# Layer 1 of a gated mixer: tokens normalised and transposed on the chip instead of column means and row scaling, and the whole program in a hand-written order

## The chip, the cores and the metric

The kernel runs on one core of a Trainium2 chip. The metric is the device time of one execution in microseconds (us); before the change it is 401.55 us (median of three runs, 401.23 to 402.5). Engines are called as the profile calls them: PE multiplies matrices (PEld loads its weights), DVE and ACT work on vectors, POOL is the general engine, and SP only issues transfers (DMAs). Each engine takes its instructions in the order of its own queue.

## What is computed

The input is 2048 tokens of 448 columns. An MLP mixer `b` and a state-space convolution `a` are mixed by a gate per token:

```python
g = sigmoid((x * gate_w).sum(-1, keepdims=True))
a = ssm(x)                         # long convolution, plus x * D_skip
h = gelu(layernorm(x) @ w1)        # layer 1: 448 -> 448
hs = concat(shift(h0, +1), shift(h1, -1), shift(h2, +2), shift(h3, -2)) @ w2
x1 = x + hs
b = x1 + gelu(layernorm(x1) @ w3) @ w4    # layer 2: 448 -> 1792 -> 448
out = g * a + (1 - g) * b
```

`layernorm` subtracts the token's mean and divides by the root of its variance; `shift` moves a quarter of the columns along the tokens by one or two places.

## The kernel before

The tokens are cut into 4 **blocks** of 512 (`TB`), a block into 4 **tiles** of 128. The work is a list of 72 **units**: 16 of layer 1 (block by block, the column groups 0, 2, 1, 3), then 56 of layer 2 (block by block, 14 groups of 128 hidden columns). A unit n has a **first product** (`first`, L378), 11 matmuls of 512 columns that leave a group of hidden columns in PSUM, then a gelu on ACT (L394, L396), its split in a rounded high part `uh` (L402, ACT) and a low part `ul` (L406, DVE), and a **second product** (`second`, L433), 12 matmuls that add the group to four sums of a tile each. All products use high and low parts of both factors, so inputs and weights are split in the same way: the high part by an ACT copy, the low part by a DVE (or POOL) subtraction.

**Step** n of the loop issues the first product of unit n+2 and the second product of unit n, and between them whatever tables `before`, `between`, `after` and `late` hold for n. They are filled by `at(n, fn, ...)`: `sp3(c, k)` splits half a chunk of `w3` (L216, L217), `sp4` two groups of `w4`, `stats_b` and `rstd` the statistics of the layer norm, `norm` and `norm_t` the normalising and transposing of a tile for layer 2 (L320, L334), `ssm_moment` and others the state-space part, whose scans run on DVE from step 28.

Layer 1 of before needs no normalised tokens. The mean over the columns is taken out of `w1` (`col_means`, L630, and `split_w1`, L634), the raw transposed tokens `xT` come from memory and are split (`split_xt`, L309 and L311), and what comes out of the first product is scaled per token by `rb` (L393). `rb` holds the tokens' reciprocal deviations as rows: `rstd_rows` (L294) transposes them on PE. The program up to step 27 is written in an order that a scheduler may change; from step 28 (`OWN`) the written order holds on each engine.

Of the kernel before, what the change touches and what calls it, by code (L numbers as in the profile page):

```python
# [31 lines left out]
OWN = 28  # L32
# [12 lines left out]
def gated_mix_kernel(tc, x, xT, w1, w2, w3, w4, par, logdt, dskip, ident, parg, uflip, lags, out):  # L45
    nc = tc.nc
    with tc.tile_pool(name="keep", bufs=1) as keep:
        xs = keep.tile([128, L // 128, D], F32, name="xs")
        gg = keep.tile([128, L // 128], F32, name="gg")
        okm = keep.tile([128, 16], I32, name="okm")  # L50
        with ExitStack() as ctx:
            mixer_and_small_steps(ctx, tc, xs, gg, okm, x, xT, w1, w2, w3, w4, par, logdt, dskip, ident, out)
# [121 lines left out]
def mixer_and_small_steps(ctx, tc, xs, gg, okm, x, xT, w1, w2, w3, w4, par, logdt, dskip, ident, out):  # L174
# [69 lines left out]
    nc.gpsimd.memset(cm, 1.0 / D)  # L244
    w1r = big.tile([128, 4, 4, GW], F32, name="w1r", tag="w4al")
    w2r = big.tile([G, 4, D], F32, name="w2r", tag="w4ah")
    raw[0] = room([128, 4, XW], "raw")
    nc.scalar.dma_start(w1r[:, 0], w1[:, 0])
    for k in range(4):
        nc.sync.dma_start(raw[0][:, k, :], xT[:, k, 0:XW])  # L250
    nc.sync.dma_start(w1r[:, 2], w1[:, 2])
    load_x(0, 1)
    load_x(1, 3)
    nc.sync.dma_start(w1r[:, 1], w1[:, 1])
    load_x(3, NT + 1)
    nc.sync.dma_start(idt, ident)
    nc.sync.dma_start(w1r[:, 3], w1[:, 3])
    nc.sync.dma_start(w2r, w2)
    load_xt(1)
    load_x(NT + 1, 2 * NT + 1)  # L260
    nc.gpsimd.memset(one, 1.0)
    nc.gpsimd.memset(nu, 0.0)
    nc.gpsimd.memset(zero, 0.0)
    nc.gpsimd.memset(carry, 0.0)
    nc.gpsimd.memset(rb[:, 0:HALO], 0.0)
    nc.gpsimd.memset(rb[:, L + HALO:L + 2 * HALO], 0.0)


    def stats_b(j0, j1):
        b6 = wk.tile([128, NT + 1, 6], F32, name="b6")  # L270
        for j in range(j0, j1):
            nc.vector.bn_stats(b6[:, j - j0, :], xs[:, j, :])  # L272
        for j in range(j0, j1):
            nc.vector.bn_aggr(st[:, j, :], b6[:, j - j0, :])

    def rstd(r, j0, j1):

        v, t = (wk.tile([128, NT + 1], F32, name=n)[:, :j1 - j0] for n in "vt")
        y = r[:, j0:j1]
        nc.vector.tensor_scalar(v, st[:, j0:j1, 1], EPS, None, op0=OP.add)  # L280
        nc.vector.tensor_scalar(y.bitcast(I32), v.bitcast(I32), -0.5, float(0x5f3759df), op0=OP.mult, op1=OP.add)
        for _ in range(3):
            nc.vector.tensor_mul(t, y, y)
            nc.vector.scalar_tensor_tensor(t, t, -0.5, v, op0=OP.mult, op1=OP.mult)
            nc.vector.scalar_tensor_tensor(y, t, 1.5, y, op0=OP.add, op1=OP.mult)

    def rstd2(j0, j1):
        rstd(r2, j0, j1)
        nc.vector.scalar_tensor_tensor(nm[:, j0:j1], st[:, j0:j1, 0], -1.0, r2[:, j0:j1], op0=OP.mult, op1=OP.mult)

    def rstd_rows(j0, j1, bank="misc"):
        p = ps.tile([128, TB], F32, name="misc", tag=bank, bufs=2 if bank == "misc" else 1)
        for j in range(j0, j1):
            nc.tensor.transpose(p[:, (j - j0) * 128:(j - j0 + 1) * 128], r1[:, j:j + 1].to_broadcast([128, 128]), idt)  # L294
        nc.scalar.activation(rb[:, HALO + j0 * 128:HALO + j1 * 128], p[:, :(j1 - j0) * 128], AF.Copy)
# [8 lines left out]
    def split_xt(b, k0, k1):  # L304
        if k0 == 0:
            hl_tiles(("a", b))
        h, lo = XH["a", b], XL["a", b]
        for k in range(k0, k1):
            nc.scalar.activation(h[:, k, :], raw[b][:, k, :], AF.Copy)  # L309
            if k < 3:  # L310
                nc.vector.tensor_sub(lo[:, k, :], raw[b][:, k, :], f32(h[:, k, :]))  # L311
            else:
                nc.vector.tensor_sub(h[64:, 3, :], raw[b][64:, 3, :], f32(h[64:, 3, :]))

    XN = {}

    def norm(b, i, early=False):
        j = NT * b + i
        xn = XN[b, i] = wk.tile([128, 512], F32, name="xn", tag="xn")
        nc.scalar.activation(xn[:, :D], xs[:, j, :], AF.Identity, bias=nm[:, j:j + 1], scale=r2[:, j:j + 1])  # L320
        if early:
            nc.vector.tensor_copy(xn[:, D:], xn[:, D - 64:D])
        else:
            nc.scalar.activation(xn[:, D:], xs[:, j, D - 64:], AF.Identity, bias=nm[:, j:j + 1], scale=r2[:, j:j + 1])

    def norm_t(b, i):
        j = NT * b + i
        if i == 0:
            hl_tiles(("d", b))
        h, lo = XH["d", b], XL["d", b]  # L330
        xn = XN.pop((b, i))
        p = ps.tile([128, 4, 128], F32, name="misc")
        for k in range(4):
            nc.tensor.transpose(p[:, k, :], xn[:, k * 128:(k + 1) * 128], idt)  # L334
        t = slice(i * 128, (i + 1) * 128)
        nc.scalar.activation(h[:, :, t], p, AF.Copy)
        NT_[b, i] = p

    NT_ = {}

    def norm_lo(b, i):
        h, lo, p, t = XH["d", b], XL["d", b], NT_.pop((b, i)), slice(i * 128, (i + 1) * 128)
        nc.vector.tensor_sub(lo[:, :, t], p[:, :3, :], f32(h[:, :3, t]))
        nc.vector.tensor_sub(h[64:, 3, t], p[64:, 3, :], f32(h[64:, 3, t]))

# [11 lines left out]
    def first(n, bank="p1", fill=0):  # L357
# [11 lines left out]
        p = P1[n] = ps.tile([128, TB], F32, name="p1", tag=bank, bufs=2)  # L369
# [7 lines left out]
        for q, (a_, b_) in enumerate(seq):  # L377
            nc.tensor.matmul(p[:m], a_, b_, start=(q == 0), stop=(q == len(seq) - 1))  # L378
            if q < 4:
                warm_up(fill)  # L380

    def act_head(n, later=False):
        kind, b, i = units[n]
        m = G if kind == "a" else 128
        lo = UL[n] = wk.tile([128, TB], F32R, name="ul", bufs=3)
# [3 lines left out]
        if kind == "a":  # L389
            if i == 0 or (i == 1 and b == NB - 1):  # L390
                logits(p, b, i)
            o = b * TB + HALO - SHIFT[i]
            nc.vector.tensor_mul(u[:m], p[:m], rb[:m, o:o + TB])  # L393
            nc.scalar.activation(u[:m], u[:m], AF.Gelu_apprx_tanh)  # L394
        else:
            nc.scalar.activation(u[:m], p[:m], AF.Gelu_apprx_tanh)  # L396
        if not later:
            act_copy(n)
# [17 lines left out]
    def second(n):  # L416
# [64 lines left out]
    def ssm_par(q):  # L481
        pk[q] = room([128, 2, 4, NS], f"pk{q}")
        nc.sync.dma_start(pk[q], par[:, 2 * q:2 * q + 2])

    def ssm_exp(q):
        nc.scalar.activation(pk[q][:, :, 0, :], pk[q][:, :, 0, :], AF.Exp)
        if q:
            return
# [4 lines left out]
    CM = {}  # L493
# [7 lines left out]
    def ssm_moment(k, m):  # L501
# [5 lines left out]
        w = wk.tile([128, 2, NS], F32, name="w", tag="xn")  # L507
        nc.vector.tensor_mul(w, c, t[:, 0:2, :])  # L508
        nx = wk.tile([128, 2, NS], F32, name="nx", tag="u")
# [29 lines left out]
    def ssm_load(b):  # L539
        ZS[b] = wk.tile([128, 4, TB], F32, name="zs", tag="rawc" if b % 2 else "rb", bufs=1)  # L540
# [45 lines left out]
    def ssm_queue():  # L586
# [6 lines left out]
        ssm_load(0)  # L593
        ssm_load(1)
# [25 lines left out]
    def run(when, n):  # L620
        for fn, a in when.pop(n, []):
            fn(*a)


    pm = ps.tile([128, 4, G], F32, name="pm", tag="misc")

    def col_means(g):
        for k in range(4):
            r = 64 if k == 3 else 128
            nc.tensor.matmul(pm[:, g, :], cm[:r].to_broadcast([r, 128]), w1r[:r, g, k, :G],  # L630
                             start=(k == 0), stop=(k == 3))

    def split_w1(g):
        nc.vector.tensor_tensor(w1r[:, g, :, :G], w1r[:, g, :, :G], pm[:, None, g, :].to_broadcast([128, 4, G]),  # L634
                                OP.subtract)
        split(w1h[:, g], w1l[:, g], w1r[:, g], nc.gpsimd if g else None)

    w4p, w3r = {}, {}
# [7 lines left out]
    def ld3(c):  # L646
        t = cols3(c)
        w3r[c] = stage([128, 4, t.stop - t.start], w3[:, :, t])
# [177 lines left out]
```

## Time and profile before

| what | value |
|---|---|
| median of three runs | 401.55 us |
| the profiled execution: time | 402.19 us |
| the profiled execution: span, first to last instruction | 400.4 us |
| granted clock, mean | 0.996 |
| PE busy, share of the span | 388.0 us, 97% |
| DVE busy | 307.1 us, 77% |
| ACT busy | 203.2 us, 51% |
| POOL busy | 57.2 us, 14% |
| start of the first product of unit 0 | 9.78 us |
| start of the first product of unit 4 (the first of block 1) | 32.95 us |
| start of the first product of unit 16 (the first of layer 2) | 97.31 us |
| end of the last second product | 393.54 us |

The span lacks some 1.8 us of the execution's time, which lie around it. A row of the profile gives line, engine, operation, output<-inputs, the shape, how often, the busy time and the mean of one in ns; a row of a timeline gives start, duration, engine, line and so on; L numbers are lines of the kernel before unless a text says "new line".

### The profile page before, as it was taken

The page shows a single profiled execution, that of the slowest core. Times are in us where ns is not written, and L with a number is a line of the kernel's source. Part 1 is how long each engine was busy: PE and PEld are TensorE (multiplying, and loading weights), DVE is VectorE, ACT ScalarE, POOL GpSimd, SP SyncE. Part 2 cuts the span into 40 slices and gives each one's busy share as a digit, 9 for nine tenths or more (in the row PEclk, how much of TensorE's full clock was granted, in tenths as well). Part 3 has the DMA queues.
Part 4 walks back from the last instruction along what each step waited for, and adds up shares of the span by engine and source line. Part 5 has one row for each costly group of instructions (what it writes and reads, how often), then busy time and mean ns, then how long its engine had stood idle before and what let it go on. Part 6 is the DMA issues. An engine that isn't in the chain of part 4 may idle for free.

```text
span 400.4 us, 5167 instructions
## 1 busy us (share of the span) xinstructions
PE 388.0 (97%) x1851; PEld 330.3 (82%) x1851; DVE 307.1 (77%) x581; ACT 203.2 (51%) x340; POOL 57.2 (14%) x127
## 2 busy tenths in 40 slices
PE   7999899999999999999999999999999999999993
PEld 3678788788888888888888888888888888888892
DVE  3689999989983387289999795997778778788222
ACT  4183667595696532275556524566266334442120
POOL 1260000000000000043025321242133301000000
PEclk9999999999999999999999999999999999999998
DMA  8991523613453000000000150000052002000002
GB/s 267 315 362 35 190 83 130 206 46 77 167 145 66 2 0 2 1 0 2 1 2 0 46 152 0 0 2 1 31 127 42 2 0 93 0 0 2 0 1 97
DMA packets 12903, 26.93 MB, mean 67 GB/s; under 512 B 1094, under 2 KB 6358, under 8 KB 12618
## 3 DMA queue, kind: packets, MB, share of 16 engines
q1 hardware_dynamic: 12730, 26.33, 21.2%
q8 instruction: 16, 0.26, 0.3%
q10 hardware_dynamic: 144, 0.23, 0.2%
q14 instruction: 13, 0.11, 0.1%
HBM read 22.88 MB, written 3.68 MB: 66 GB/s over the span
## 4 chain that ended last, share of the span: by engine, by line
PE 87%; DVE 6%; DMA 2%; ACT 2%; issue 1%; DVEq 0%; ACTq 0%
PE p L378 41%; PE acc L433 40%; PE misc L334 2%; PE misc L570 2%; DMA raw<-w_in 1%; DVE b L272 1%; DMA w1r<-w_in 1%; DVE ul L406 1%; PE pw L666 1%; PE pm L630 1%; DVE xl L311 1%; PE misc L294 1%; DVE w3l L217 1%; DVE uf L393 1%; ACT xh L309 0%
## 5 line engine op out<-in xcount | busy, mean ns | idle before, releaser
L396 ACT ACTIVATE uf<-p 128x512 f32<-128x512 f32 x56 | 33.5, 598 | 141.8 <-PE p L378 138.0
L406 DVE TENSOR_TENSOR ul<-uf,uh 128x512 fp32r<-128x512 f32 (+1 forms) x72 | 50.7, 705 | 36.6 <-ACT uh L402 36.4
L378 PE MATMUL p<-xh,w3h 128*128 128x512 f32 x224 | 61.2, 395 | 0.0
L378 PE MATMUL p<-xh,w3l 128*128 128x512 f32 x224 | 60.8, 393 | 0.0
L433 PE MATMUL acc<-w4h,uh 128*128 128x448 f32 x224 | 59.9, 372 | 0.0
L558 DVE TENSOR_TENSOR_SCAN z<-z,carry,zero 128x512 f32<-128x512 f32 x48 | 59.9, 1269 | 0.0
L433 PE MATMUL acc<-w4h,ul 128*128 128x448 f32 x224 | 58.2, 364 | 0.0
L433 PE MATMUL acc<-w4l,uh 128*128 128x448 f32 x224 | 58.1, 364 | 0.0
L378 PEld LDWEIGHTS p<-xh,w3l 128*128 128x128 f32 x224 | 42.1, 188 | 9.9
L378 PE MATMUL p<-xl,w3h 128*128 128x512 f32 x168 | 47.9, 394 | 0.0
L378 PEld LDWEIGHTS p<-xh,w3h 128*128 128x128 f32 x224 | 42.1, 188 | 6.7
L560 POOL COPY carry<-z 128x1 f32<-128x1 f32 x60 | 28.0, 470 | 137.1 <-DVE z L558 136.0
L402 ACT ACTIVATE uh<-uf 128x512 fp32r<-128x512 f32 (+1 forms) x72 | 45.4, 631 | 1.5
L433 PEld LDWEIGHTS acc<-w4l,uh 128*128 128x128 f32 x224 | 42.0, 188 | 3.2
L433 PEld LDWEIGHTS acc<-w4h,ul 128*128 128x128 f32 x224 | 42.0, 188 | 3.2
L433 PEld LDWEIGHTS acc<-w4h,uh 128*128 128x128 f32 x224 | 40.6, 188 | 4.4
L558 DVE TENSOR_TENSOR_SCAN z<-z,carry 128x512 f32<-128x512 f32 x32 | 41.0, 1283 | 2.0
L548 ACT ACTIVATE z<-zs,nu 128x512 f32<-128x512 f32 x64 | 41.0, 713 | 0.0
L547 POOL COPY z<-carry 128x1 f32<-128x1 f32 x48 | 20.6, 473 | 136.1 <-DVE w L508 107.3
L378 PEld LDWEIGHTS p<-xl,w3h 128*128 128x128 f32 x168 | 31.5, 188 | 7.3
L578 DVE SCALAR_TENSOR_TENSOR xs<-misc,gg,xs 128x448 f32<-128x448 f32 x16 | 10.2, 678 | 13.6 <-PE misc L570 13.6
L433 PE MATMUL acc<-w2h,uh 112*128 112x448 f32 x64 | 19.9, 371 | 0.0
(121 smaller groups left out, 493.4 us busy)
## 6 DMA issues: line engine op xcount, KB each, us to landing
zs<-xT_in SPq DMA_DIRECT2D x4, 1024.0 KB, 6.4
out_dram<-xs SPq DMA_DIRECT2D x16, 224.0 KB, 2.0
raw<-xT_in SPq DMA_DIRECT2D x3, 1032.0 KB, 11.7
raw<-w_in SPq DMA_DIRECT2D x3, 1024.0 KB, 5.5
raw<-w_in SPq DMA_DIRECT2D x3, 896.0 KB, 4.9
pk<-par_in SPq DMA_DIRECT2D x2, 1024.0 KB, 5.9
xs<-x_in SPq DMA_DIRECT2D x2, 896.0 KB
raw<-xT_in SPq DMA_DIRECT2D x4, 258.0 KB, 4.5
```

The lines of the kernel that those rows point to most:

```text
L334: nc.tensor.transpose(p[:, k, :], xn[:, k * 128:(k + 1) * 128], idt)
L378: nc.tensor.matmul(p[:m], a_, b_, start=(q == 0), stop=(q == len(seq) - 1))
L396: nc.scalar.activation(u[:m], p[:m], AF.Gelu_apprx_tanh)
L402: nc.scalar.activation(UH[n][:m], UF[n][:m], AF.Copy)
L406: nc.vector.tensor_sub(UL[n][:m], UF.pop(n)[:m], f32(UH[n][:m]))
L433: nc.tensor.matmul(ACC[j], (UL if p == 2 else UH)[n][:m, t], wl if p == 1 else wh, start=s and p == 0, stop=e and p == 2)
L547: nc.gpsimd.tensor_copy(z4[:, m, 0:1], carry[:, k, m:m + 1])
L548: nc.scalar.activation(z4[:, m, 1:], ZS[b][:, k, :], AF.Copy, scale=nu[:, k, m:m + 1])
L558: nc.vector.tensor_tensor_scan(z, z, up, carry[:, k, m:m + 1], OP.add, OP.add)
L560: nc.gpsimd.tensor_copy(carry[:, k, m:m + 1], z[:, TB - 1:])
L570: nc.tensor.transpose(p[:, k * 128:(k + 1) * 128], ZS[b][:, k, i * 128:(i + 1) * 128], idt)
L578: nc.vector.scalar_tensor_tensor(r, p[:, :D], gg[:, j:j + 1], r, op0=OP.mult, op1=OP.add)
```

## The change

Layer 1 is done as layer 2 is: each tile is normalised (`norm`, ACT, with a copy of 64 columns on POOL), transposed on PE (`norm_t`, four 128x128 transposes), and split (`norm_hi`, `norm_lo`). `cm`, `col_means`, `rb`, `rstd_rows`, `split_xt`, the row scaling and the loads of `xT` for layer 1 go. The shifts reach over a block's edge by two columns: `halo` copies them between neighbouring blocks on POOL (four small copies each time), `edge` fills the two outer ends with zeros on ACT. The gate's logit is now read from a product with normalised tokens, so `gates` puts it back (three DVE operations, and the sum of `gate_w`, which `gate_sum` loads and adds). The low parts of `w1` and `w2` are taken on DVE, not POOL. Layer 1 has its own statistics (`st1`, `r1`, `nm1`).

The whole program is put under the written order, where before only the steps from 28 were. In a step the order is now: `ul` of unit n+1, `before`, first product and gelu of unit n+2, `between`, copy to `uh`, `after`, the scans' share, `late`, second product of unit n. `stats`, `rstd` and `ln` are generators, which `mix` deals out in turn; what isn't a generator in a table is issued first. The scaling of the first scan step, which stood ahead of the mask that fills `nu` (at 136.65 us, the mask's last instruction at 172.19 us), is put behind it.

```diff
+    def norm(kind, b, i, eng):
+        ...
+        nc.scalar.activation(xn[:, :D], xs[:, j, :], AF.Identity, bias=m[:, j:j + 1], scale=r[:, j:j + 1])
+        if eng is nc.scalar:
+            nc.scalar.activation(xn[:, D:], xs[:, j, D - 64:], AF.Identity, bias=m[:, j:j + 1], scale=r[:, j:j + 1])
+        else:
+            eng.tensor_copy(xn[:, D:], xn[:, D - 64:D])
...
+    def norm_lo(kind, b, i):
+        h, lo, p, t = XH[kind, b], XL[kind, b], PT.pop((kind, b, i)), cols(kind, i)
+        nc.vector.tensor_sub(lo[:, :, t], p[:, :3, :], f32(h[:, :3, t]))
+        nc.vector.tensor_sub(h[64:, 3, t], p[64:, 3, :], f32(h[64:, 3, t]))
+
+    def halo(b):
+        for X in (XH, XL):
+            u, v = X["a", b - 1], X["a", b]
+            nc.gpsimd.tensor_copy(u[:, :, TB + HALO:], f32(v[:, :, HALO:2 * HALO]))
+            nc.gpsimd.tensor_copy(v[:, :, :HALO], f32(u[:, :, TB:TB + HALO]))
...
-            nc.vector.tensor_mul(u[:m], p[:m], rb[:m, o:o + TB])
-            nc.scalar.activation(u[:m], u[:m], AF.Gelu_apprx_tanh)
+        nc.scalar.activation(u[:m], p[:m], AF.Gelu_apprx_tanh)
...
+    def gate_sum():
+        t = wk.tile([128, D], F32, name="gt", tag="uf")
+        nc.sync.dma_start(t, gateb)
+        nc.vector.tensor_reduce(sg, t, axis=AX.X, op=OP.add)
...
-    warm_up(5)
-    col_means(0)
-    split_w1(0)
-    split_xt(0, 0, 4)
-    warm_up(3)
-    first(0, fill=2)
+    warm_up(28)
...
+    mix([stats(st1, 0, 4)])
+    nc.scalar.activation(w1h[:, 0], w1r[:, 0], AF.Copy)
+    mix([rstd(st1, r1, nm1, 0, 4)])
...
+    for i in range(4):
+        norm("a", 0, i, nc.gpsimd)
+        norm_t("a", 0, i, banks[i])
+        warm_up(1)
+        if i < 2:
+            norm_hi("a", 0, i, False)
+            norm_lo("a", 0, i)
+    for i in (2, 3):
+        norm_hi("a", 0, i)
+        norm_lo("a", 0, i)
+    first(0)
...
+    for b, n in ((2, 2), (3, 5)):
+        h = NT * b + (2 if b > 2 else 0)
+        if b > 2:
+            at(n, stats, st1, NT * b, h)
+        at(n + (b > 2), ln, st1, r1, nm1, NT * b, h, NT * b + 4)
+        for i in range(NT):
+            n = 4 * b - 5 + i // 2
+            at(n, norm, "a", b, i, nc.gpsimd, when=before)
+            n = 4 * b - 5 + i // 2 * 2
+            at(n, norm_t, "a", b, i, when=between)
+            at(n, norm_hi, "a", b, i, when=between)
+            at(n, norm_lo, "a", b, i, when=late)
+            if i == 0:
+                at(n, halo, b, when=late)
+    at(9, edge, 3, TB + HALO)
...
+    for c, m0, m1, n, w in ((0, 4, 6, None, None), (2, 12, 13, 7, "raw"), (1, 9, 11, None, None), (3, 14, 15, 11, "raw")):
+        if w:
+            at(n, ld3, c, w)
+        at(m0, sp3, c, 0)
+        at(m1, sp3, c, 2)
...
-    with tc.manual_schedule():
-        for n in range(OWN, len(units)):
+    for n in range(len(units)):
```

What the order of the instructions is, at three places. The first is DVE where the statistics of the last block of layer 1 become reciprocal deviations. Before, the chain (L280 to L285, `r_82` or `r_83`) is threaded between other rows: the split of `w3` (L217), the row scaling (L393), the low part `ul` (L406).

```order
L272 BN_STATS b_678<-xs 128x6
L284 SCALAR_TENSOR_TENSOR t<-t,v 128x4 [waits DVE_49]
L217 TENSOR_TENSOR w3l<-raw,w3h 128x2x512 [waits DMAHW7_49]
L393 TENSOR_TENSOR uf<-p_558,rb 112x512 [waits Activation_49]
L285 SCALAR_TENSOR_TENSOR r_82<-t,r_82 128x4 [waits DVE_49]
L274 BN_AGGR st<-b_678 128x2
L217 TENSOR_TENSOR w3l<-raw,w3h 128x2x512
```

Now, in step 6, one half chunk of `w3` stands first, and waits for ACT; two tiles' statistics and then the whole chain (new lines 267 to 278, twelve operations) follow without anything between.

```order
L402 TENSOR_TENSOR ul<-uf,uh 112x512 [waits Activation_49]
L218 TENSOR_TENSOR w3l<-raw,w3h 128x2x512 [waits Activation_49]
L257 BN_STATS b_674<-xs 128x6 x2
L260 BN_AGGR st_78<-b_674 128x2 [waits DVE_49] x2
L267 TENSOR_SCALAR v<-st_78 128x4 [waits DVE_49]
L269 TENSOR_SCALAR r_85<-v 128x4 [waits DVE_49]
L272 TENSOR_TENSOR t<-r_85 128x4 [waits DVE_49]
```

So the chain, whose result the tiles 12 and 13 are normalised with, moved behind a split whose high part comes from ACT. The second place is ACT in the same steps. Before, between the gelu of a unit (L394) and its `uh` (L402) stand the high parts of the raw tokens (L309) and the rows `rb` (L295); `p_558` is unit 8's.

```order
L295 ACTIVATE rb<-misc 128x512 [waits PE_49]
L394 ACTIVATE uf<-uf 112x512 [waits DVE_49]
L309 ACTIVATE xh<-raw 128x516
L402 ACTIVATE uh<-uf 112x512 [waits Activation_49]
L458 ACTIVATE lr<-p_558 18x512 [waits PE_49]
```

Now (`p_652` is unit 8's) the high part of `w3` comes behind gelu, logit rows and `uh` of unit 8, and the normalising of tiles 12 and 13 (new line 308) behind that, ahead of the gelu of unit 9.

```order
L392 ACTIVATE uf<-p_652 112x512 [waits DVE_49,PE_49]
L456 ACTIVATE lr<-p_652 18x512 [waits Pool_49]
L398 ACTIVATE uh<-uf 112x512 [waits Activation_49]
L217 ACTIVATE w3h<-raw 128x2x512
L308 ACTIVATE xn<-xs,nm_79,r_85 128x448 [waits DMAHW0_49,DVE_49,Pool_49]
L308 ACTIVATE xn<-xs,nm_79,r_85 128x448 [waits DMAHW0_49,Activation_49]
L392 ACTIVATE uf<-p_712 112x512 [waits PE_49]
```

So in this stretch ACT no longer has loaded tokens to split, and its normalising stands between two units. The third place is PE between the first product of unit 9 and the second product of unit 7. Before (`p_601` is unit 9's, `acc_500` the first tile's sum of block 1), the one followed the other:

```order
L378 MATMUL p_601<-xh,w1h 112x512 x3
L378 MATMUL p_601<-xh,w1l 112x512 x4
L378 MATMUL p_601<-xl,w1h 112x512 x3
L433 MATMUL acc_500<-w2h,uh 128x448 [waits Activation_49]
L433 MATMUL acc_500<-w2l,uh 128x448
```

Now the same kind of first product (`p_712`, unit 9) is followed by the transposes of tiles 12 and 13 (new line 324), each waiting for ACT and for POOL's copy, and the second product of unit 7 (`acc_584`) comes behind them.

```order
L383 MATMUL p_712<-xh,w1h 112x512 x4
L383 MATMUL p_712<-xh,w1l 112x512 x4
L383 MATMUL p_712<-xl,w1h 112x512 x3
L324 MATMUL misc<-idt,xn 128x128 [waits PE_49,Activation_49]
L324 MATMUL misc<-idt,xn 128x128 x2
L324 MATMUL misc<-idt,xn 128x128 [waits Pool_49]
L431 MATMUL acc_584<-w2h,uh 128x448
```

What moved into PE's queue is a wait for another engine's product in the middle of a step.

More of the change, by code (lines that the diff above doesn't have):

```diff
@@ L31 @@
 LAG = 2
-OWN = 28
 RHO = 1.0 / 64.0
@@ L243, in mixer_and_small_steps @@
     nc.gpsimd.memset(warm, 0.0)
-    nc.gpsimd.memset(cm, 1.0 / D)
+    nc.gpsimd.memset(zero, 0.0)
+    nc.gpsimd.memset(one, 1.0)
+    nc.gpsimd.memset(nu, 0.0)
+    nc.gpsimd.memset(carry, 0.0)
     w1r = big.tile([128, 4, 4, GW], F32, name="w1r", tag="w4al")
     w2r = big.tile([G, 4, D], F32, name="w2r", tag="w4ah")
[L247 to L250, printed above, removed]
+    nc.scalar.dma_start(idt, ident)
@@ L291, in rstd_rows @@
[L291 to L295, printed above, removed]
+            yield
+        nc.vector.scalar_tensor_tensor(m[:, j0:j1], s[:, j0:j1, 0], -1.0, y, op0=OP.mult, op1=OP.mult)
@@ L315, in mixer_and_small_steps @@
[L315 to L332 removed]
+    XN, PT = {}, {}
@@ L620, in run, with ld3 @@
     def run(when, n):
[L621 to L631, printed above, removed]
+        mix([fn(*a) for fn, a in when.pop(n, [])])
+    w4p, w3r = {}, {}
     def split_w1(g):
[L634 to L638, printed above, removed]
+        split(w1h[:, g], w1l[:, g], w1r[:, g])
     def sp2(g):
-        split(w2h[:, g, :], w2l[:, g, :], w2r[:, g, :], nc.gpsimd)
+        split(w2h[:, g, :], w2l[:, g, :], w2r[:, g, :])
     def cols3(c):
         return slice(c * 512, min((c + 1) * 512, F))
-    def ld3(c):
+    def ld3(c, where):
         t = cols3(c)
-        w3r[c] = stage([128, 4, t.stop - t.start], w3[:, :, t])
+        w3r[c] = stage([128, 4, t.stop - t.start], w3[:, :, t], where)
     def sp3(c, k):
@@ new lines, in mixer_and_small_steps, with rest @@
+    nc.scalar.activation(w1h[:, 1], w1r[:, 1], AF.Copy)
+    for j in (5, 6, 7):
+        bn(j)
+    for j in range(4, 8):
+        nc.vector.bn_aggr(st1[:, j, :], b6[:, j - 4, :])
+    first(1)
+    act_head(0)
+    act_copy(0)
+    def rest():
+        nc.vector.tensor_tensor(w2l[:, 0], w2r[:, 0], f32(w2h[:, 0]), OP.subtract)
+        yield
+        yield
+        yield
+        act_tail(0)
+        yield
+        yield
+        sp2(2)
+    mix([rstd(st1, r1, nm1, 4, 8), rest()])
+    second(0)
@@ new lines, in mixer_and_small_steps, with tiles45 @@
+    act_head(1)
+    act_copy(1)
+    for i in range(2):
+        norm("a", 1, i, nc.gpsimd)
+    act_tail(1)
+    nc.vector.tensor_tensor(w1l[:, 1], w1r[:, 1], f32(w1h[:, 1]), OP.subtract)
+    def tiles45():
+        for i in range(2):
+            norm_t("a", 1, i)
+            norm_hi("a", 1, i)
+            norm_lo("a", 1, i)
+            if i == 0:
+                halo(1)
+    second(1, tiles45)
+    for i in (2, 3):
+        norm("a", 1, i, nc.gpsimd)
+    split_w1(3)
+    first(2)
+    act_head(2)
```

298 lines of the change are left out of this document (148 added, 150 removed).

## The prediction

> **What bounds the kernel now.** I read the summary by engine first, then the shares of the chain that ended last, then the timeline of PE.
>
> ```profile
> PE 388.0 (97%) x1851; PEld 330.3 (82%) x1851; DVE 307.1 (77%) x581; ACT 203.2 (51%) x340; POOL 57.2 (14%) x127
> PE 87%; DVE 6%; DMA 2%; ACT 2%; issue 1%; DVEq 0%; ACTq 0%
> 32.95 1.11 PE L378 MATMUL p<-xh,w1h 128*114 128x512 f32 x4
> 41.48 0.62 PE L294 MATMUL misc<-idt,r 128*128 128x128 f32 x4 [1.29 <-DVE st L274]
> 41.85 0.71 PE L378 MATMUL p<-xl,w1h 128*112 128x512 f32 x2
> 91.90 1.10 PE L378 MATMUL p<-xh,w1h 128*112 128x512 f32 x4
> 94.46 0.60 PE L334 MATMUL misc<-idt,xn 128*128 128x128 f32 x4
> 94.81 1.05 PE L433 MATMUL acc<-w2h,uh 112*128 112x448 f32 x4
> 97.31 1.09 PE L378 MATMUL p<-xh,w3h 128*128 128x512 f32 x4
> ```
>
> PE bounds it. A first product takes 94.46 - 91.90 = 2.56 us, a tile's four transposes 94.81 - 94.46 = 0.35, the second product behind them 97.31 - 94.81 = 2.50. From 32.95 (first product of unit 4) PE has one marked wait, 1.29 us at 40.2. So I cut the run there and at 97.31 (first product of unit 16): stage 1 is 32.95 us, stage 2 64.36, stage 3, to the span's end, 400.40 - 97.31 = 303.09. DVE is the second bound, in stage 2 above all:
>
> ```profile
> 40.00:50.00 10.00, 8.71 (x44) 7.48 (x44) 10.00 (x43) 6.63 (x10) 0.00 (x0) 1.00 0.51 191
> ```
>
> The third number is PE's busy time, the fifth (before its count) DVE's: it is full. It costs PE little, since rows of DVE that nobody waits for are mixed among those that are waited for. Under the written order a queue can no longer do that.
>
> **Stage 1, new: about the same length.** The prices:
>
> ```profile
> raw<-xT_in SPq DMA_DIRECT2D x4, 258.0 KB, 4.5
> 0.75 4.07 DMA w1r<-w_in
> 5.00:6.00 1.00, 1.00 (x5) 1.00 (x6) 0.69 (x1) 0.87 (x2) 0.00 (x0) 1.00 1.03 299
> L272 DVE BATCH_NORM_STATS2 b<-xs 128x6 f32<-128x448 f32 x32 | 19.0, 616 | 0.1
> L274 DVE BATCH_NORM_AGGREGATE st<-b 128x2 f32<-128x6 f32 x32 | 4.8, 169 | 0.0
> 201.46 0.16 DVE L280 TENSOR_SCALAR v<-st 128x4 f32<-128x4 f32 x1
> 203.65 0.16 DVE L289 SCALAR_TENSOR_TENSOR nm<-st,r 128x4 f32<-128x4 f32 x1
> L320 ACT ACTIVATE xn<-xs,nm,r 128x448 f32<-128x448 f32 x16 | 11.9, 753 | 3.2 <-DVE nx L515 3.2
> L560 POOL COPY carry<-z 128x1 f32<-128x1 f32 x60 | 28.0, 470 | 137.1 <-DVE z L558 136.0
> L322 DVE COPY xn<-xn 128x64 f32<-128x64 f32 x8 | 1.5, 194 | 2.3 <-ACT xn L320 2.3
> L217 POOL TENSOR_TENSOR w1l<-w1r,w1h 128x456 fp32r<-128x456 f32 x3 | 3.5, 1172 | 18.8 <-ACT w1h L216 18.8
> L336 ACT ACTIVATE xh<-misc 128x512 fp32r<-128x512 f32 x16 | 9.5, 593 | 0.3 <-PE misc L334 0.3
> L343 DVE TENSOR_TENSOR xl<-misc,xh 128x384 fp32r<-128x384 f32 x16 | 8.9, 554 | 2.8 <-ACT xh L336 2.5
> L344 DVE TENSOR_TENSOR xh<-misc,xh 64x128 fp32r<-64x128 f32 x16 | 4.7, 294 | 0.2
> ```
>
> Some 0.5 MB (228 KB and one 258 KB piece) has landed at 4.82; identity and four tiles are 1.0 MB, so the fourth tile lands 0.5 MB at 299 GB/s later, at 6.4. Its statistics (0.6), four aggregates (0.5) and the chain of twelve operations (203.81 - 201.46 = 2.35) end at 9.9; normalising (0.75), POOL's copy and the transposes at 11.5. POOL's copy of 64 columns is in no row: from 0.2 us (the same copy on DVE, L322) to 1.2 (POOL's subtraction of 456 columns); I take 0.5, by the nearest of POOL's own, its copies of one column at 0.47. Then DVE paces: two high parts from PSUM at 0.6 (as L336) and four tiles' low parts at 0.85 (554 + 294), 4.6 in all, to 16.1, where the fourth matmul of unit 0 can start; that product ends at 18.1, the next at 20.6. Then PE has two second products (5.0), two first products (5.1) and four tiles' transposes (1.4), and waits some 0.9 for the statistics of tiles 4 to 7 and for the halo: **33.0**, against 32.95. Bounds: 30.5 (POOL at 0.2, its part in series four times, and those waits and half of DVE's excess hidden) and 36 (POOL at 1.2, four times in series).
>
> **Stage 2, new.** Out: three groups of row transposes (0.36 each, 41.85 - 41.48), 1.0 us, and the wait of 1.29. In: the transposes of blocks 2 and 3, 8 x 0.35 = 2.8. The row scaling (L393) and `xT`'s splitting leave DVE and ACT, which PE did not wait for. Then the waits. Prices:
>
> ```profile
> L394 ACT ACTIVATE uf<-uf 112x512 f32<-112x512 f32 x16 | 10.0, 628 | 12.2 <-DVE uf L393 12.2
> L458 ACT ACTIVATE lr<-p 18x512 f32<-18x512 f32 x5 | 3.0, 592 | 7.7 <-PE p L378 7.7
> L402 ACT ACTIVATE uh<-uf 128x512 fp32r<-128x512 f32 (+1 forms) x72 | 45.4, 631 | 1.5
> 66.18 1.06 ACT L216 ACTIVATE w3h<-raw 128x1024 fp32r<-128x1024 f32 x1 [0.44 <-DMA raw<-w_in]
> 62.52 1.22 DVE L217 TENSOR_TENSOR w3l<-raw,w3h 128x1024 fp32r<-128x1024 f32 x1
> L406 DVE TENSOR_TENSOR ul<-uf,uh 128x512 fp32r<-128x512 f32 (+1 forms) x72 | 50.7, 705 | 36.6 <-ACT uh L402 36.4
> out_dram<-xs SPq DMA_DIRECT2D x16, 224.0 KB, 2.0
> ```
>
> *Tiles 12 and 13, step 7: 4.0.* From the end of unit 8's first product, one after the other: gelu 0.63, logit rows 0.59, `uh` 0.63, high part of `w3` 1.06, its low part 1.22, two statistics 1.2, two aggregates 0.3, chain 2.35, two normalisings 1.5, POOL's copy 0.5: 10.0, less some 0.6 by which neighbours on one engine overlap, 9.4. PE meanwhile has a second product (2.50), a first product (2.56) and the first tile's transposes (0.35), 5.4. Behind the waiting transposes stand the second product of unit 7 and all that follows.
>
> *Block 3's first product, step 10: 2.5.* From the end of unit 11's first product: gelu 0.63, two high parts 1.19, `uh` 0.63, two zero fills of 0.15, high and low part of `w3` 2.28, low parts of tiles 14 and 15 1.7: 6.7, less 0.3. PE has two tiles' transposes, a second product and three matmuls (0.7, three elevenths of a product) before the fourth, which reads the last low part: 3.9.
>
> *Tiles 8 and 9, step 3: 1.5.* DVE comes from tile 7's low part with two `w2` splits, two `ul`, four statistics and the chain: 0.6 x 2 + 0.6 x 2 + 2.2 + 0.5 + 2.35 = 7.5, then two normalisings and the copy, 2.0, from about 33.0; PE has 2.56 + 2.50 + 2.56 + 0.35 = 8.0. Bounds 0 and 4.
>
> *The sum of the gate's weights, step 11: 0.6.* Its load (224 KB, 2.0 us as `out_dram`'s) starts when a `uf` is free, and DVE waits for it ahead of the four additions on which unit 12's second product waits. Bounds 0 and 2.5.
>
> Stage 2: 64.36 - 1.0 - 1.29 + 2.8 + 8.6 = **73.5**.
>
> **Stage 3, new.** Same units, same scans. Two waits more:
>
> ```profile
> L348 ACT ACTIVATE xs<-xs,gs 128x448 f32<-128x448 f32 x16 | 10.5, 658 | 0.0
> L216 ACT ACTIVATE w4h<-raw 128x896 fp32r<-128x896 f32 x7 | 6.5, 944 | 1.1 <-PE p L378 1.1
> L486 ACT ACT_TABLE_LOAD x2 | 2.6, 1283 | 0.0
> L486 ACT ACTIVATE pk<-pk 128x512 f32<-128x512 f32 x2 | 1.3, 632 | 1.3 <-DMA pk<-par_in 1.2
> 144.81 0.69 DVE L508 TENSOR_TENSOR w<-nx,pk 128x512 f32<-128x512 f32 x1
> 147.27 0.69 DVE L508 TENSOR_TENSOR w<-nx,pk 128x512 f32<-128x512 f32 x1
> ```
>
> In step 20 ACT has gelu, `uh`, `w4` (0.94), a weighing (0.66), a table load (1.28), the exponential (0.63), then tiles 4 and 5 of layer 2 (1.5) and POOL's copy: 6.8, less 0.6, while PE has 5.4: 0.8, and 2.3 if the gelu waits in turn for DVE. I take 1.6. In steps 18 and 24 DVE has two moments (147.27 - 144.81 = 2.46 each), statistics and a chain (3.7) and an `ul` (0.7), 9.3 us in a step of 5; what is left over reaches unit 26's `ul`: 0.5, bounds 0 and 2.5. Stage 3: 303.09 + 2.1 = **305.2**.
>
> **The sum.** 33.0 + 73.5 + 305.2 = 411.7 us of span. The profiled execution took 402.19 for a span of 400.4, so 413.5; the median of before lies 0.6 below its profiled execution: **412.9**.
>
> [...] PE starts at half pace:
>
> ```profile
> 1.34 2.31 PE L666 MATMUL pw<-warm 128*128 128x512 bf16 x5 [1.34 <-POOL cm L244]
> 9.78 1.70 PE L378 MATMUL p<-xh,w1h 128*114 128x512 f32 x3
> 12.43 1.11 PE L378 MATMUL p<-xh,w1l 128*114 128x512 f32 x4
> ```
>
> The matmuls at 1.34 come every 0.44 us, those at 12.43 every 0.24; the three at 9.78 are still slow, with the granted clock at 1.00 throughout. The 28 new filling matmuls take 12.2 us at the slow pace and end between 9 and 13.5; from there to 16 PE has only sixteen transposes and four fillers. If it falls back to half pace there, the first two products cost up to 22 x 0.20 = 4.4 more; some of it lies beside DVE's work, so 2 to 4. [...]
>
> **Rivals.**
>
> *Only the two longest waits reach PE*: these two follow from the order alone; the other four rest on how far DVE is behind. 33.0 + 71.4 + 303.1 = 407.5, time 408.7.
>
> *Half pace in the prologue*, above: 415 to 417.
>
> *No wait reaches PE*, because DVE and ACT run ahead: 33.0 + 64.9 + 303.1 = 401.0, time 402.2. Against it: the tile 12 path is 9.4 us beside 5.4.
>
> *Faster: an early start.* The gelus no longer wait for rows of reciprocal deviations, and POOL's long subtractions are gone. If the start of unit 4 comes at 30.5 and no wait reaches PE, the time is 30.5 + 64.9 + 303.1 + 1.1 = 399.6. It decides for faster where start plus all new waits of PE come below 31.2, and with the two longest waits (6.5) the start would have to come before 24.7: the chain of loads, DVE's splits and PE's products above can't be that short.
>
> **How the numbers follow.** The forecast (410 to 415) 0.57, only two waits (407 to 410) 0.20, half pace or a later start (415 to 418) 0.12, no wait (401 to 404) 0.07, early 0.04. The range 406.5 to 417.5 leaves out some 0.15. A measurement can tell 0.3% (1.2 us) from no change: faster 0.04; within 0.3%, most of the no-wait case, 0.05; slower 0.91.
>
> **What would show it.** The start of unit 4's first product at 33; PE waiting some 4 us ahead of the transposes of tile 12, in the middle of step 7, released by ACT or POOL after DVE's chain; some 2.5 us inside block 3's first product, released by the second low part of tile 15; PE's waits from there to unit 16 and to unit 28 of 1 to 3 us. I would be wrong if ACT took `w3` or `w4` earlier than its queue says, or if the filling matmuls end after 13.5.

## The result and the profile after

The changed kernel takes 417.67 us (median of four runs, 416.81 to 420.37) against 401.75 for the kernel before: a ratio of 1.0406, with a 95% interval from 1.0355 to 1.0457. So it is slower, by some 16 us. The forecast was 412.9 with a range up to 417.5: the sign was right, the time came 4.8 us above the forecast, and it lies 0.2 above the range, which is less than the four runs differ among themselves. The profiled execution took 418.04 for a span of 416.2.

The summary by engine and the shares of the chain that ended last, of the changed kernel:

```profile
PE 394.8 (95%) x1883; PEld 334.2 (80%) x1883; DVE 309.7 (74%) x586; ACT 211.7 (51%) x353; POOL 56.5 (14%) x153
PE 65%; DVE 12%; ACT 3%; issue 2%; DMA 1%; SPq 0%
```

The chain was on PE for 87% of the span before, and for 65% now: DVE and ACT have more of it. (The shares that this row lists add up to 83%.) PE's waits, in the view of waits (engine, line, what it waited for, total, how often, longest):

```profile
PE misc L324 <- ACT xn L308: 7.4, 4, 3.7
PE p L383 <- DVE xh L336: 3.5, 2, 2.2
PE acc L431 <- ACT uf L392: 0.7, 1, 0.7
PE acc L431 <- DVE xs L437: 0.6, 1, 0.6
PE acc L431 <- DVE ul L402: 0.3, 1, 0.3
PE p L383 <- POOL xh L342: 0.3, 1, 0.3
```

The same waits stand in PE's timeline at the places that the prediction named (start, duration, operation; in brackets the idle time ahead and who ended it). Units 4 and 16, at which the stages are cut, are among the rows:

```profile
16.34 0.49 PE L383 MATMUL p<-xh,w1h 128*114 128x512 f32 x1 [1.25 <-DVE xh L336]
33.06 1.12 PE L383 MATMUL p<-xh,w1h 128*114 128x512 f32 x4
41.43 1.31 PE L324 MATMUL misc<-idt,xn 128*128 128x128 f32 x8 [0.64 <-ACT xn L308]
67.20 1.97 PE L324 MATMUL misc<-idt,xn 128*128 128x128 f32 x8 [3.73 <-ACT xn L308]
87.18 0.49 PE L383 MATMUL p<-xh,w1h 128*114 128x512 f32 x1 [2.24 <-DVE xh L336]
101.60 0.47 PE L431 MATMUL acc<-w2h,uh 112*128 112x448 f32 x1 [0.63 <-DVE xs L437]
109.10 1.10 PE L383 MATMUL p<-xh,w3h 128*128 128x512 f32 x4
148.78 1.53 PE L324 MATMUL misc<-idt,xn 128*128 128x128 f32 x8 [1.72 <-ACT xn L308]
177.99 1.08 PE L431 MATMUL acc<-w4h,ul 128*128 128x448 f32 x4 [0.28 <-DVE ul L402]
197.44 0.44 PE L431 MATMUL acc<-w4h,uh 128*128 128x448 f32 x1 [0.67 <-ACT uf L392]
```

Stage 1 ends at 33.06, stage 2 at 109.10, the span at 416.2:

| stage | before | forecast | after |
|---|---|---|---|
| 1, to unit 4's first product | 32.95 | 33.0 | 33.06 |
| 2, to unit 16's first product | 64.36 | 73.5 | 76.04 |
| 3, to the end of the span | 303.09 | 305.2 | 307.10 |
| span | 400.4 | 411.7 | 416.2 |

Stage 2 has fewer microseconds of waits than forecast (0.64 + 3.73 + 2.24 + 0.63 = 7.24, forecast 8.6), and is still longer. What is behind the wait of 3.73 shows where. First PE's rows there, and then the same work one pair of tiles earlier:

```profile
62.62 0.85 PE L383 MATMUL p<-xl,w1h 128*112 128x512 f32 x3
67.20 1.97 PE L324 MATMUL misc<-idt,xn 128*128 128x128 f32 x8 [3.73 <-ACT xn L308]
68.81 0.72 PE L431 MATMUL acc<-w2h,uh 112*128 112x448 f32 x1
73.29 1.09 PE L383 MATMUL p<-xh,w1h 128*114 128x512 f32 x4
...
52.48 1.03 PE L324 MATMUL misc<-idt,xn 128*128 128x128 f32 x8
53.27 1.06 PE L431 MATMUL acc<-w2h,uh 112*128 112x448 f32 x4
55.77 1.11 PE L383 MATMUL p<-xh,w1h 128*114 128x512 f32 x4
```

Two tiles' transposes and a second product take 55.77 - 52.48 = 3.29 us there, and 73.29 - 67.20 = 6.09 behind the wait: 2.80 more. The windows of the same stretch (length, busy time of PE, PEld, DVE, ACT and POOL, then the granted clock of PE, where 1.00 is full speed, the DMA share and GB/s) say why:

```profile
65.50:66.00 0.50, 0.00 (x0) 0.00 (x0) 0.40 (x4) 0.00 (x0) 0.00 (x0) 1.00 0.96 377
66.00:66.50 0.50, 0.00 (x0) 0.00 (x0) 0.47 (x3) 0.12 (x1) 0.00 (x0) 0.77 1.05 410
72.50:73.00 0.50, 0.50 (x3) 0.46 (x2) 0.44 (x1) 0.00 (x0) 0.00 (x0) 0.50 0.00 0
73.00:73.50 0.50, 0.50 (x3) 0.40 (x3) 0.20 (x2) 0.00 (x0) 0.00 (x0) 0.90 0.00 0
...
414.00:415.00 1.00, 0.00 (x0) 0.00 (x0) 0.00 (x0) 0.00 (x0) 0.00 (x0) 0.72 0.00 0
```

The granted clock falls from 1.0 to 0.5 while PE waits, at 66.27 (a mean of 0.77 over 66.0 to 66.5 is 0.27 us at 1.0 and 0.23 at 0.5), and comes back at 73.10. PE works at half pace from 67.20 to 73.10.

So the theory was: the wait for tile 12 cost 3.73 us by itself and some 2.8 by the clock that it let fall, and only the first was in the sum. The rivals: the slow stretch comes from something else at that place (the transposes, or the load that runs beside it at 400 GB/s), or DVE simply has more work in steps 6 to 12 than it can do, so that no order would help.

### The profile page after: what moved, and what is told of

The parts are those of the page before. It is cut to its first block, busy times and chain, and to the rows that moved or that the text cites. A ratio compares the mean times of both kernels' runs of the same rounds, so it can differ in the third digit from the quotient of the medians.

```text
span 416.2 us, 5296 instructions
## 1 busy us (share of the span) xinstructions
PE 394.8 (95%) x1883; PEld 334.2 (80%) x1883; DVE 309.7 (74%) x586; ACT 211.7 (51%) x353; POOL 56.5 (14%) x153
## 4 chain that ended last, share of the span: by engine, by line
PE 65%; DVE 12%; ACT 3%; issue 2%; DMA 1%; SPq 0%
PE acc L431 31%; PE p L383 31%; DVE mw L517 2%; PE misc L579 2%; PE misc L324 1%; DVE ul L402 1%; DVE mw L519 1%; DVE xl L335 1%; DVE mw L524 1%; DVE mw L522 1%; DVE b L257 1%; DVE w4l L218 1%; DVE mw L523 1%; ACT uf L392 1%; DVE xh L336 1%
## 5 line engine op out<-in xcount | busy, mean ns | idle before, releaser
L392 ACT ACTIVATE uf<-p 128x512 f32<-128x512 f32 (+1 forms) x72 | 43.1, 598 | 172.3 <-PE p L383 160.6
L402 DVE TENSOR_TENSOR ul<-uf,uh 128x512 fp32r<-128x512 f32 (+1 forms) x72 | 49.1, 684 | 20.2 <-ACT uh L398 19.9
L569 POOL COPY carry<-z 128x1 f32<-128x1 f32 x60 | 29.2, 490 | 131.7 <-DVE z L567 130.6
L308 ACT ACTIVATE xn<-xs,nm,r 128x448 f32<-128x448 f32 x32 | 22.9, 752 | 10.6 <-issue 7.9
L335 DVE TENSOR_TENSOR xl<-misc,xh 128x384 fp32r<-128x384 f32 x32 | 17.8, 555 | 11.8 <-ACT xh L329 11.3
L312 POOL COPY xn<-xn 128x64 f32<-128x64 f32 x24 | 7.0, 294 | 142.6 <-ACT xn L308 142.4
```

Source lines behind the costliest of these rows:

```text
L402: nc.vector.tensor_sub(UL[n][:m], UF.pop(n)[:m], f32(UH[n][:m]))
L569: nc.gpsimd.tensor_copy(carry[:, k, m:m + 1], z[:, TB - 1:])
```

## The experiments

**Filling the wait (`e1_fill12`).** Twelve filling matmuls stand in the wait; what PE waits for doesn't change.

```diff
+    def fill_pe(m):
+        p = ps.tile([128, TB], F32, name="misc")
+        for _ in range(m):
+            nc.tensor.matmul(p, warm[:, 0:128], warm[:, :TB], start=True, stop=True)
...
+    at(7, fill_pe, 12, when=between)
```

> The changed kernel with twelve filling matmuls (512 columns, as in the prologue) in PE's queue of step 7, between the first product of unit 9 and the transposes of tile 12; nothing else differs. They take 12 x 0.21 = 2.6 us at full pace and stand inside the wait of 3.73 us, so some 1.1 us of it stays idle and the transposes come no earlier. Theory A (the idle wait itself lowers the granted clock to 0.5, which cost 6.09 us for what takes 3.29 at full pace, 2.8 us): no stretch from 62 to 75 with a granted clock below 1.0, time 417.7 - 2.8 = 414.9 (414 to 416). Theory B (the slow stretch comes from something else at that place, the transposes themselves or the load that runs at over 400 GB/s then): the slow stretch stays, time 417.7 or up to 0.5 more.

Measured: 416.15 us (415.88 to 417.23). PE's timeline there and at step 21, and the windows of step 21:

```profile
66.96 1.31 PE L324 MATMUL misc<-idt,xn 128*128 128x128 f32 x8 [1.12 <-ACT xn L308]
70.52 1.07 PE L383 MATMUL p<-xh,w1h 128*114 128x512 f32 x4
146.21 1.54 PE L324 MATMUL misc<-idt,xn 128*128 128x128 f32 x8 [1.72 <-ACT xn L308]
...
148.00:149.00 1.00, 1.00 (x4) 0.89 (x3) 0.93 (x4) 0.99 (x3) 0.00 (x0) 0.55 1.15 209
150.00:151.00 1.00, 1.00 (x4) 0.88 (x4) 1.00 (x3) 1.00 (x4) 0.00 (x0) 0.50 0.61 236
151.00:152.00 1.00, 1.00 (x5) 0.90 (x4) 0.96 (x4) 0.80 (x3) 0.00 (x0) 0.74 0.04 14
```

The transposes of tile 12 come when they came (66.96), and the work behind them takes 70.52 - 66.96 = 3.56 us in place of 6.09, without a slow window. Unit 16 starts at 106.53 instead of 109.10. So the idle wait, not the transposes or the load, let the clock fall: theory A. That is 2.53 won, not 2.80, since the second tile's transposes still wait for their own input here (68.02 - 66.96 = 1.06 for both tiles, not 0.79). The median fell by 1.5 only, and is 0.15 above theory A's range. In this execution another wait, the 1.72 us of step 21, was followed by 3.4 us of half clock (148.10 to 151.52), and the way from these transposes to the next first product took 151.59 - 146.21 = 5.38 us; the trace of the changed kernel has the same wait of 1.72, full clock behind it, and 152.60 - 148.78 = 3.82.

**A split of `w3` out of the way, one step later (`e2_w3late`).**

```diff
-    for c, m0, m1, n, w in ((0, 4, 6, None, None), ...
+    for c, m0, m1, n, w in ((0, 4, 7, None, None), ...
```

> The changed kernel with the second half of w3's chunk 0 split in step 7 instead of step 6. Its high part (1.06 on ACT) and low part (1.22 on DVE) go out of the chain to tile 12. Theory A (order made the wait and the wait made the slow clock): wait 3.73 - 2.3 = 1.4 us, no slow stretch, time 417.7 - 2.3 - 2.8 = 412.6 (411.5 to 414). Theory B (slow clock not from the wait): 417.7 - 2.3 = 415.4. Rival C (the split only comes due later, and PE waits at block 3's first product or at the second product of unit 8 instead): 416 to 418.

Measured: 415.99 us (414.19 to 416.6). The timelines of DVE, POOL and PE:

```profile
66.72 1.23 DVE L218 TENSOR_TENSOR w3l<-raw,w3h 128x1024 fp32r<-128x1024 f32 x1 [5.44 <-ACT w3h L217]
67.97 0.56 DVE L335 TENSOR_TENSOR xl<-misc,xh 128x384 fp32r<-128x384 f32 x1
68.98 0.19 POOL L342 CAST xh<-xh 128x8 fp32r<-128x8 f32 x1 [6.72 <-DVE xh L336]
69.22 1.10 PE L383 MATMUL p<-xh,w1h 128*114 128x512 f32 x3 [2.34 <-POOL xh L342]
```

The wait for tile 12 is gone, wholly. But now the low part of tile 12 stands behind the split, the halo of block 3 behind that, and PE waits 2.34 us for the halo one unit later; the clock falls there (69.86 to 73.28), and once more behind the wait of step 21 (148.38 to 151.78). Rival C, with a gain of 1.7.

**The chain first, then the split (`f1_chain`).** Both stay in step 6, in the other order.

```diff
+    def behind(fn, *a):
+        for _ in range(20):
+            yield
+        fn(*a)
...
-        at(m1, sp3, c, 2)
+        if c:
+            at(m1, sp3, c, 2)
+        else:
+            at(m1, behind, sp3, c, 2)
```

> The changed kernel with one thing in step 6 turned round: the second half of w3's chunk 0 is split behind the statistics and the chain of block 3, not ahead of them. Theory (DVE's order in step 6 makes the wait for tile 12, and the wait makes the slow clock): that wait falls from 3.73 to at most 1.0 and no half clock follows it: 417.7 - 2.7 to 3.7 - 2.8 = 411.2 to 412.2, or 1.5 more where the wait of step 21 falls into one window of the clock, as in e1_fill12 and e2_w3late. Rival (the 1.22 us on DVE only come due later, at unit 8's low part or at the halo of block 3, as in e2_w3late): a new wait of over 1 us between 64 and 75, time 414 to 416.

Measured: 413.21 us (411.11 to 415.4). DVE's timeline first of the changed kernel and then of this one (L278 is the chain's last row):

```profile
61.42 1.23 DVE L218 TENSOR_TENSOR w3l<-raw,w3h 128x1024 fp32r<-128x1024 f32 x1 [4.74 <-ACT w3h L217]
62.56 1.15 DVE L257 BATCH_NORM_STATS2 b<-xs 128x6 f32<-128x448 f32 x2
66.14 0.16 DVE L278 SCALAR_TENSOR_TENSOR nm<-st,r 128x4 f32<-128x4 f32 x1
```

```profile
56.75 1.15 DVE L257 BATCH_NORM_STATS2 b<-xs 128x6 f32<-128x448 f32 x2
60.33 0.16 DVE L278 SCALAR_TENSOR_TENSOR nm<-st,r 128x4 f32<-128x4 f32 x1
61.57 1.23 DVE L218 TENSOR_TENSOR w3l<-raw,w3h 128x1024 fp32r<-128x1024 f32 x1 [1.08 <-ACT w3h L217]
```

In the changed kernel DVE stood idle for 4.74 us in front of the split, waiting for ACT, with the whole chain behind it. With the chain ahead, its last row comes 5.8 us earlier and the split only 0.15 later. PE has no marked wait from 41.59 to 80.62. The transposes of tiles 12 and 13 and the second product behind them take 66.74 - 63.47 = 3.27 us. Unit 16 starts at 102.61, 6.49 us earlier than in the changed kernel, and that is the 3.73 of the wait and the 2.80 of the clock (6.53). The medians differ by less, 4.46: the profiled run, with a mean granted clock of 0.998, is the best one at 411.11, just below the range that the theory gave without half clock at step 21; the other three have clocks of 0.983 to 0.988 and take 412.54 to 415.4, and this trace does not show where they lost it.

**One split of step 9 later (`e3_c3late`).**

```diff
-    ... (1, 9, 11, None, None) ...
+    ... (1, 10, 11, None, None) ...
```

> The changed kernel with the first half of w3's chunk 1 split in step 10 instead of step 9, behind the low parts of tiles 14 and 15. If DVE's order in step 9 makes the wait of 2.24 us in block 3's first product: that wait falls to under 1.1 and the time by 1.2 to 2.2, to 415.5 to 416.5; the slow stretch after step 7 stays. Rival: the split is then late for units 12 and 13 (ul, tile 0 and 1 of layer 2) and the wait only moves one step on: 417.7 within 0.7.

Measured: 418.35 us (416.95 to 418.55). PE's timeline:

```profile
86.75 0.49 PE L383 MATMUL p<-xh,w1h 128*114 128x512 f32 x1 [0.28 <-DVE xh L336]
102.47 0.47 PE L431 MATMUL acc<-w2h,uh 112*128 112x448 f32 x1 [1.93 <-DVE xs L437]
```

Block 3's wait falls from 2.24 to 0.28, so its cause is as predicted, the split ahead of the last low parts on DVE. But the wait of step 11 grows from 0.63 to 1.93: DVE still waits for the gate's weights ahead of the additions and comes to them 0.86 later (101.79 for 100.93), and PE is there 0.44 earlier. So the time is the rival's, 417.7 within 0.7, not the 415.5 to 416.5 of the theory: most of the wait moved one place on. The gain of 0.66 in these two is less than what the profiled execution loses to a slow stretch in its prologue (16.54 to 19.94).

**All four rows put right (`f2_order`).** The chain first; the split of step 9 behind the low parts; the gate's weights loaded in step 3 and added in step 13; the second exponential in step 18.

```diff
...
-        at(m0, sp3, c, 0)
+        at(m0, sp3, c, 0, when=late if c == 1 else after)
...
-    at(11, gate_sum)
+    at(3, gate_in)
+    at(13, gate_sum)
...
-    at(20, ssm_exp, 1)
+    at(18, ssm_exp, 1)
```

> f1_chain with three more rows moved: the first half of w3's chunk 1 behind the low parts of tiles 14 and 15 in step 9; the load of the gate's weights in step 3 into a buffer of its own and their sum in step 13; the second exponential of the state-space part in step 18 instead of 20. Theory (each wait is made by one row that stands too early in a queue): block 3's wait 2.24 to under 0.5, step 11's 0.63 to 0, step 21's 1.72 to under 0.5, beside f1_chain's: 417.7 - 3.2 - 2.8 - 2.0 - 0.6 - 1.5 = 407.6 (406 to 409.5). Rival (DVE has more work than fits from step 6 to 12, so that its waits only gather at the next row of it that PE needs): 410 or more, with a wait of over 2 us somewhere from 64 to 110.

Measured: 407.77 us (407.62 to 409.82). Of stage 2 only the 0.64 and 0.29 us are left, of step 21 0.32 and 0.19. But in step 26 a wait has grown:

```profile
169.95 1.08 PE L431 MATMUL acc<-w4h,ul 128*128 128x448 f32 x4 [1.49 <-DVE ul L402]
```

It was 0.28 in the changed kernel. Behind step 21 PE is 9.25 us earlier than in the changed kernel, but DVE's low part, behind moments, statistics and a chain, comes only 8.04 earlier (169.20 for 177.24); DVE is busy for 28.64 of the 30 us from 140 to 170. That is the overload of DVE that the prediction had put at 0.5, with a bound of 2.5, and it takes back 1.2 us of what was won at step 21. Four of the five runs have clocks of 0.997 or 0.998 and lie within 407.62 to 408.25, as the theory said (407.6); the fifth, at 0.993, took 409.82, and is the profiled one: half clock from 16.86 to 20.28, in the prologue. So DVE has not more work in steps 6 to 12 than it can do.

**The change without its order.** The written order is taken away, first up to step 27 (`e4_sched`), then for steps 2 to 27 alone (`f3_sched2`, which opens it ahead of the prologue, closes it at step 2 and opens it again at step 28). The edit of the first:

```diff
-            ctx.enter_context(tc.manual_schedule())
...
+        if n == 28:
+            own.enter_context(tc.manual_schedule())
```

> The changed kernel, but the written order holds only from step 28 on, as in the kernel before; up to there the scheduler may change the order. This is the half of the change that normalises and transposes layer 1's tokens, without the other half, the written order. Theory (the written order of steps 2 to 27 made the waits, the normalising only adds transposes): of the waits of stages 2 and 3 (7.2 and 2.7), the slow stretch (2.8) and what follows little is left: 403 to 408. Rival (the normalised layer 1 itself loads ACT and DVE so much that PE waits in any order): above 411.

> The changed kernel with the written order for the prologue and from step 28 on; steps 2 to 27 may be reordered by the scheduler. Theory (the normalised layer 1 costs little in itself; e4_sched's longer time lies in its prologue, where all sixteen transposes went ahead of unit 0): unit 4 starts at 33 as in the changed kernel, stage 2 is 64.4 - 1.0 - 1.3 + 2.8 + 0.5 = 65.4, stage 3 303.6 as in e4_sched: span 402.1, time 403.9 (403 to 406). Rival (stage 2 itself is longer with the normalising in any order): unit 16's first product behind 101, time above 407.

Measured: 408.66 us (408.09 to 410.46) and 406.15 (406.14 to 406.95). PE's first transposes in the changed kernel; then its transposes and its first product of unit 0 in the first of these runs; then the first product of units 4 and 16 in the second one:

```profile
10.61 0.66 PE L324 MATMUL misc<-idt,xn 128*128 128x128 f32 x4 [1.35 <-ACT xn L308]
...
13.46 3.73 PE L323 MATMUL misc<-idt,xn 128*128 128x128 f32 x16 [2.46 <-ACT xn L307]
17.87 2.27 PE L382 MATMUL p<-xh,w1h 128*114 128x512 f32 x7 [0.69 <-ACT xh L328]
...
33.80 1.12 PE L382 MATMUL p<-xh,w1h 128*114 128x512 f32 x4
100.34 1.10 PE L382 MATMUL p<-xh,w3h 128*128 128x512 f32 x4
```

The first is 0.7 above the range that the theory gave, and loses in the prologue. Not because sixteen transposes run ahead of unit 0, as the expectation of the second run has it: they do so in the changed kernel too. They come later (13.46 in place of 10.61, since ACT normalises from 12.66 on and not from 9.80), behind a wait of 2.46 us, and at half clock up to 16.84. Unit 4 starts at 36.45 there. With the written prologue it starts at 33.80, stage 2 takes 66.54 and stage 3 404.3 - 100.34 = 303.96; the longest wait of PE behind unit 4 is 0.69 us. So the rest of the change, the normalising above all, costs 404.3 - 400.4 = 3.9 us of span (0.85 + 2.18 + 0.87), and the written order of steps 2 to 27, with the clock that its waits let fall, the other 416.2 - 404.3 = 11.9. The second run is 0.15 above its range, and its unit 16 starts at 100.34, below the 101 of its rival: that the normalised layer 1 is too much for DVE and ACT in any order does not hold. At 1.0116 of the kernel before (1.0094 to 1.0138) this is the fastest version with the normalising, and still slower than the kernel before. The written order without the normalising was not run.

**The changed kernel again (`f4_after`).**

> The changed kernel once more, unaltered, for its spread and a second trace: 417.7 (416.5 to 420.5). [...] If the wait alone decides, only that of 3.7 us is followed by half clock and the runs agree within 0.3 us.

Measured: 417.76 us (416.97 to 418.7). The waits came at the same places (3.71, 2.25, 0.86 and 1.71 us), and again only the longest was followed by half clock, from 65.72 to 72.56. The trace by itself is as it would be if the wait alone decided; but the four runs differ by 1.7 us and not by 0.3, and the wait of step 21, 1.71 here and 1.72 in the first trace with full clock behind it, was followed by half clock in `e1_fill12` and `e2_w3late`. Over the eight runs of the changed kernel the fastest (416.81) has the highest clock, 0.994, and the slowest (420.37) the lowest, 0.979; the five at 0.990 lie between 416.97 and 418.04.

## Why the prediction was wrong

**The step that failed** is the term "4.0" for the tiles 12 and 13. The wait was right (3.73), its place and cause too, but the sum let PE go on at full pace behind it. The prediction knew of half pace, saw it in the first ten microseconds (2.31 us for five matmuls at 1.34, 1.11 for four at 12.43), and priced a fall back to it in the prologue alone, as a rival with a chance of 0.12. Of the longest gap that the prediction itself forecast, 4.0 us in step 7, the same was never asked. It cost 2.5 to 2.8 us, shown by the filled wait (transposes at the same time, 3.56 in place of 6.09) and by the turned order (3.27 in place of 6.09, and unit 16 earlier by 6.49 for 3.73 + 2.80 = 6.53). By the prediction's own sum, 412.9 + 2.8 = 415.7, inside the range; most of the rest is in the smaller sizes below.

**Right, within a few tenths:** unit 4's start (33.06 for 33.0), with unit 0's fourth matmul at 16.34 for 16.1; block 3's first product (2.24 for 2.5); the sum of the gate's weights (0.63 for 0.6); step 21, which the prediction called step 20 for the rows on ACT that make it (1.72 for 1.6); unit 26's low part (0.28 for 0.5). The four rows named as causes were the right ones: with them moved, the waits went or fell to 0.5 us or less. Part of this is luck. The 1.6 of step 21 was taken between a sum of 0.8 and 2.3. And in stage 1 errors offset each other: POOL's copy takes 0.24 us (median) for 0.5, a high part on DVE 0.69 for 0.6, two tiles' transposes 0.79 for 0.7, and from unit 0 to unit 4 only one wait, of 0.26, is marked for 0.9.

**Sizes that were off:** the wait of tiles 8 and 9 is 0.64 for 1.5. The three groups of row transposes that went are 3 x 0.37 = 1.1 by the prediction's own rows, not 1.0. Two tiles' transposes in one piece take 0.79 us (53.27 - 52.48), not twice 0.35: 0.09 for each of the six pairs of stage 2, and again for the six of stage 3, some 0.5 each. At 41.43 and 148.78 the second tile's transposes wait once more for their own input, which the marked waits don't hold: 42.50 - 41.43 = 1.07, and 1.29 from 148.78 to the second product at 150.07, where 0.79 would do. With these, stage 2 is accounted for to 0.3 us (2.80 - 1.36 for the waits + 0.54 + 0.28 = 2.26 of 2.54) and stage 3 as well (0.57 for the waits + 0.54 + 0.50 = 1.61 of 1.90).

**Missed:** the wait of 0.67 us at 197.44. ACT's timeline of the changed kernel shows eight scalings of the state-space part in one piece ahead of a gelu:

```profile
188.91 5.00 ACT L557 ACTIVATE z<-zs,nu 128x512 f32<-128x512 f32 x8
193.82 0.57 ACT L392 ACTIVATE uf<-p 128x512 f32<-128x512 f32 x1
```

Four of them are those that stood from 136.65 us on in the kernel before and are now put behind the mask. The same wait, 0.67 to 0.72, is in every variant; that it comes from this move is read from the rows and was not tried by itself.

**The rivals.** Half pace in the prologue did not come back in the profiled execution (granted clock 1.00 up to 66.27), but it does in some: in that of `e3_c3late` (16.54 to 19.94) unit 4 starts at 34.63, 1.6 us later than in the changed kernel. It was priced at 2 to 4. The measured time lies in this rival's band (415 to 418), but for another reason: half pace came behind step 7. The 28 filling matmuls took 7.92 us, not 12.2, and ended at 9.26. The cases without waits, and with two waits only, fall.

## What to carry to other kernels

A forecast wait of PE is priced twice: by its length, and by the clock that it may let fall. Here the wait of 3.7 us was followed by half clock in each of the three traces that have it, one of 2.34 in `e2_w3late`, and that of 1.7 at step 21 in two of six; the 2.2 us in block 3's first product never were. Under a written order a row that waits for another engine should not stand ahead of a chain that nothing holds up: DVE stood 4.74 us before a split with the chain behind it, and turning the two round won 6.5 us in the trace (4.5 in the median), while moving the split a step later only moved the wait. Where the scheduler had mixed such rows by itself (steps 2 to 27 of `f3_sched2`, 11.9 us shorter), a hand-written order has to be checked row by row at each place where one engine waits for another.

## What the runs showed of the hardware

In the changed kernel the granted clock falls at 66.27 behind the wait of 3.73 us and rises at 73.10 (6.83 us later); in `f4_after` it falls at 65.72 and rises at 72.56 (6.84). It was at half for 3.42 us behind the 2.34 of `e2_w3late` (69.86 to 73.28), and behind the wait of step 21 for 3.42 in `e1_fill12` (148.10 to 151.52) and 3.40 in `e2_w3late` (148.38 to 151.78). Behind the last product it falls as well, at 414.44 in the changed kernel and at 410.94 in the kernel with the filled wait.

The length of the wait alone does not say whether the clock falls: the 1.7 us of step 21 cost it in two of the traces (`e1_fill12`, `e2_w3late`) and not in four others, and the 2.24 us in block 3's first product, which are longer, never did. Nor does the fall come at one distance from the products: 2.80 us behind the last one in the changed kernel (63.47 to 66.27), 2.00 in `f4_after` (63.72 to 65.72), and at step 21 of `e1_fill12` 1.89 us after PE had begun again (146.21 to 148.10). What decides it no run shows; that the wait of step 21 costs the clock where it "falls into one window", as the expectation of `f1_chain` has it, was the author's estimate, and what was measured is its cost where it did: 5.38 - 3.82 = 1.56 us in `e1_fill12`.

In `e4_sched` the clock was at half from 13.42 to 16.84 (3.42 us) and PE had only transposes in that time (the row of sixteen at 13.46), and at 16.84 it went back to 1.0:

```profile
14.00:15.00 1.00, 1.00 (x6) 1.00 (x5) 0.73 (x3) 0.92 (x3) 0.24 (x1) 0.50 0.99 238
16.50:17.00 0.50, 0.50 (x5) 0.45 (x3) 0.47 (x3) 0.50 (x2) 0.02 (x1) 0.67 1.07 384
17.00:17.50 0.50, 0.18 (x2) 0.00 (x0) 0.50 (x1) 0.46 (x2) 0.00 (x0) 1.00 1.06 380
```
